# Modulation columns summed on DVE, one product for 32 rows of the special column, one load queue: a spectral block followed by an MLP

## The chip, the cores and the metric

The kernel runs on one core of a Trainium2 chip. The metric is the device time of one execution in microseconds (us). Engines are named as in the profile: PE (TensorE; PEld are its weight loads), DVE (VectorE), ACT (ScalarE), POOL (GpSimd) and SP (SyncE, which here only issues DMAs). SBUF is the core's working memory, PSUM the eight banks into which PE writes; a `bank` in the code is one of them (128 partitions x 512 float32), taken in turn from two of one tag (A, B, C or D).

## The reference

One sequence of 2048 rows by 512 columns, float32. From a condition vector c come six modulation vectors of 512: shift, scale and gate of two blocks.

```python
mod = (silu(c) @ w_mod).reshape(1, 6, 1, 512)
sa, ca, ga, sb, cb, gb = (mod[:, i] for i in range(6))
h = layernorm(x) * (1 + ca) + sa
x = x + ga * irfft2(rfft2(h) * (w_r + 1j * w_i))      # over rows and columns
h = layernorm(x) * (1 + cb) + sb
x = x + gb * (mish(h @ w1 + b1) @ w2)                 # 512 -> 1376 -> 512
```

## The kernel before

The rows are split as 128 x 16 (partition p, tile n), the columns as 128 x 4. The Fourier transforms are products with constant matrices. Where a line has high and low parts ("split"), a float32 is written as a rounded value and its rest, and three products take the place of one. A plain float32 product of 128 x 128 shows as two matmul rows of the profile, one for each pass; transposes show as one.

**Stage 1** (L291-370) goes over the 16 tiles n. `p1_row` (L203) multiplies the transposed tile by the row matrix that `scale_rows` has scaled with 1 + ca (`krs`); `p1_mean` (L213) takes the mean away on DVE, with the row sums `kb` from `row_sums` (L208); `p1_cast` (L218) makes the high part on ACT; the low part comes from POOL for n in `POOL_LOW` (1, 3, ..., 13) and otherwise from DVE in `p1_low` (L231); `p1_col` (L237) is the column product, three sets of three matmuls, of which the third takes the low part; `p1_save` (L247) is ACT's copy into `a_sb`. `norm_sums` (L111) makes a tile's statistics on DVE; `first_guess` (ACT) and `first_scale` (three DVE steps) make its 1/sigma, for two tiles at a time after the first two. `p1_split` (ACT, POOL) splits the column matrices. The order of all engines' work is written out by hand (`manual_schedule`): each engine takes its own instructions in the order of the lines, and so does each DMA queue.

Ahead of tile 0, sigmoid(c) is made with an exp on ACT and three DVE steps (`sc`, 512 values as 128 x 4), eight products of ones by ones run (`warm`, L286), and 16 products of `w_mod`'s scale part by `sc` give 1 + ca's row in four banks (`scale_sums`, L250). c and two of the four pieces of `w_mod` are loaded by ACT's queue, all else by SP's.

The shift sa enters as one more row: `shift_sum` (L261) adds four pieces of `w_mod` (`wms`), each times its column of `sc`, on DVE at tiles 10 to 13; `shift_columns` (L269) turns the 128 partial sums into columns with four products by ones (in `mod_columns`, L105); `shift_rows` (L272) multiplies the row matrix with these columns, picks each partition's own part and adds it up on DVE into `saz`. Both stand ahead of the column products of tiles 14 and 15. `saz` is added by POOL to one column of each group in stage 2 (`p2_shift`, L462).

**Stage 2** (L372-595) goes over 17 groups of frequencies, in the order `seq`; group 0, the fifth, is the special one (frequencies 0 and 256 of the columns, functions `z_*`). For each group: transposes on PE (`p2_in`, L454), a copy on ACT, `saz` on POOL, a product (`p2_mul`, L475), two DVE multiplications with the weights (`p2_prod`, L491), sums on DVE or POOL (L496, L497), transposes back (`p2_back`, L508), a copy on ACT, a product (`p2_out`, L521), and ACT's copies into `d` (`store_d`). Steps are lagged: at step s the loop makes prod(s), mul(s+1), in(s+3), back(s-2), out(s-3). Eight `p2_in` and two `p2_mul` run ahead of the loop. In the special group, `reflected` (L396) makes three matmul pairs per operand: the operand, its first column into one row, and the operand reversed. `z_back` gives two operands, 128 rows (times `kv`) and 32 rows (times `kw`).

The other four modulation vectors are summed in this stage, at most two DVE steps per loop step (`mod_late`, L98 and L100): ga into `modr[:, 0]`, sb into `modr[:, 1]`, cb into `modr[:, 0]`, gb into `modr[:, 2]`. `mod_shift` (L543) turns sb and cb into columns, each with four products by ones, at steps 11 and 18; `mod_gate` (L551) and `apply_gate` (L556) spread ga and gb.

**Stage 3** (L655-675, L898-930) is the inverse transform: `p3_col` and `p3_row` per tile on PE, the addition to x (L674) and the new statistics on DVE, with the splits of w1 and w2 in between (`split_w2`, L715; `split`, L711, is an ACT copy and a DVE subtraction, L713). For w2's tile 3, sums of pieces from POOL (`tsum` = `modr[:, 0:2]`) are split at step 14. **Stage 4** is the MLP, eight pairs of tiles, six steps each: `up` (L748, L750), `front`, `back` (mish), `halves`, `down` (L793, L801).

Of the kernel before, what the change touches and what calls it, by code (L numbers as in the profile page):

```python
# [27 lines left out]
POOL_LOW = range(1, 15, 2)  # L28
# [3 lines left out]
def tile_spectral_block(ctx: ExitStack, tc: tile.TileContext, x_d, w1_d, b1_d, w2_d,  # L32
# [36 lines left out]
    macc = modr[:, 1]  # L69
# [21 lines left out]
    kw = pw.tile([32, 384], F32, name="kw")  # L91
# [10 lines left out]
    def mod_columns():  # L102
        ps = bank("D")
        for j in range(4):
            nc.tensor.matmul(ps[:, j:j + 1], macc[:, j * P:(j + 1) * P], ones[:, 0:1], start=True, stop=True)  # L105
        return ps[:, 0:4]
# [70 lines left out]
    def load_rest():  # L177
        nc.sync.dma_start(ident, kp_d)
# [82 lines left out]
    def shift_sum(k):  # L261
        w, one = wms[:, k, :], sc[:, k:k + 1]
        if k == 0:
            st["sum"] = bank("D")
            nc.vector.tensor_scalar(st["sum"], w, one, 0.0, op0=ALU.mult, op1=ALU.add)
        else:
            nc.vector.scalar_tensor_tensor(macc if k == 3 else st["sum"], w, one, st["sum"], op0=ALU.mult, op1=ALU.add)

    def shift_columns():  # L269
        nc.scalar.mul(cols[:, 0, 0, :], mod_columns(), 128.0)  # L270

    def shift_rows():  # L272
# [5 lines left out]
        pick = modr[:, 1, 0:8]  # L278
# [12 lines left out]
    with tc.manual_schedule():  # L291
        def load_scale(eng, k):
            eng.dma_start(wmc[:, k, :], wm_d[:, 1, k, :])

        nc.scalar.dma_start(sc, c_d.rearrange("b (p k) -> p (b k)", k=4))
        load_scale(nc.scalar, 1)
        load_scale(nc.scalar, 3)
        nc.scalar.preload_act_table_set("natural_log_exp_and_others")
        load_xt(0)
        load_scale(nc.sync, 0)  # L300
        load_scale(nc.sync, 2)
        nc.sync.dma_start(kr, kr_d)
        load_x(0)
        load_m(0)
        for n in range(1, 8):
            load_all(n)
# [8 lines left out]
        warm(8)  # L315
        cps = [bank(t) for t in "CCBB"]
        for k in range(4):
            scale_sums((k,), cps)
        norm_sums(0)
        first_guess(0, 1)  # L320
        scale_rows(cps)
        first_scale(0, 1)
        p1_split(0)
        row_sums()
# [15 lines left out]
        for n in range(N2):  # L340
            if n >= 1:
                p1_save(n - 1)
            if n + 2 < N2:
                p1_row(n + 2)
                if n + 10 < N2:
                    load_all(n + 10)
                if n == 4:
                    nc.sync.dma_start(wms, wm_d[:, 0, :, :])
                if n == 6:
                    load_rest()  # L350
# [17 lines left out]
            if 10 <= n < 14:  # L368
                shift_sum(n - 10)
        p1_save(N2 - 1)  # L370

# [24 lines left out]
    def reflected(out, srcs):  # L396
        for i, (t, w) in enumerate(srcs):
            nc.tensor.matmul(out, t[:, 0:P], w(0), start=(i == 0), stop=False)
            nc.tensor.matmul(out[0:1], t[:, 0:1], w(2), start=False, stop=False)
            nc.tensor.matmul(out, t[:, P:2 * P], w(1), start=False, stop=(i == len(srcs) - 1))  # L400
# [9 lines left out]
    def z_mul():  # L410
        z = st.pop(("z", 0))
        pb = bank("B")
        reflected(pb[:, 0:160], [(z, lambda i: kf[:, 128 + 160 * i:288 + 160 * i])])
        st["pb", 0] = pb

    def z_prod():
# [10 lines left out]
        nc.gpsimd.tensor_tensor(y[:, 80:160], pr[0][:, 80:160], pr[1][:, 0:80], op=ALU.add)  # L427
        st["y", 0] = y

    def z_back():  # L430
# [3 lines left out]
        nc.tensor.transpose(pc[0:32, P:2 * P], y[:, P:P + 32], ident)  # L434
        t1, t2 = buf("t"), buf("t")
        turned(t1, pc[:, 0:P])
        turned(t2[0:32], pc[0:32, P:2 * P])
        st["t", 0] = t1, t2

    def z_out():  # L440
        t1, t2 = st.pop(("t", 0))
        pe = bank("D")
        reflected(pe[:, 0:P], [(t1, lambda i: kv[:, 128 + i * P:256 + i * P]),
                               (t2[0:32], lambda i: kw[:, i * P:(i + 1) * P])])
# [83 lines left out]
    for i, s in enumerate(when):  # L528
        work_mod[s].append((i // 4, (0, 1, 0, 2)[i // 4], nc.vector, i % 4))

    def mod_fetch(s):
        for which, row, eng, k in work_mod.get(s, ()):
            w = late[which, k] = hring.tile([P, 512], F32, name="wm", tag="ht", bufs=4)
            nc.sync.dma_start(w, wm_d[:, 2 + which, k, :])

    def mod_late(s):
        for which, row, eng, k in work_mod[s]:
            mod_step(modr[:, row], late.pop((which, k)), k, eng)

    def mod_shift(i):  # L540
        ps = bank("A")
        for j in range(4):
            nc.tensor.matmul(ps[:, j:j + 1], modr[:, 1 - i, j * P:(j + 1) * P], ones[:, 0:1], start=True, stop=True)  # L543
        if i:
            plus_one(cols[:, 1, i, :], ps[:, 0:4])
        else:
            nc.scalar.copy(cols[:, 1, i, :], ps[:, 0:4])
# [13 lines left out]
    with tc.manual_schedule():  # L561
        for i in range(8):
            nc.sync.dma_start(wqb[:, i], wq_d[8 + i])
        for i in range(LEAD):
# [4 lines left out]
            if i in (3, 5):  # L569
                p2_mul(seq[i // 2 - 1])  # L570
        for s in range(len(seq) + 3):
# [16 lines left out]
            if s == 7:  # L588
                mod_gate()
            if s == 9:  # L590
# [124 lines left out]
    def split_w2(t, sums):  # L715
# [5 lines left out]
        if sums:  # L721
# [208 lines left out]
    front(1)  # L930
    halves(0, back(0))
# [29 lines left out]
def _constants():  # L961
# [80 lines left out]
    kw = np.concatenate([m[128:] for m in zero], 1)  # L1042
# [5 lines left out]
def _layout(x, w_r, w_i, w_mod):  # L1048
# [13 lines left out]
    m = w_mod.reshape(128, 4, 6, 512).transpose(0, 2, 1, 3).copy()  # L1062
    m[:, 0:3] = m[:, 0:3].reshape(128, 3, 4, 128, 4).swapaxes(3, 4).reshape(128, 3, 4, 512)
# [31 lines left out]
```

## Time and profile before

| | us |
|---|---|
| median of 3 runs (lowest to highest) | 396.13 (395.94 to 396.22) |
| the profiled execution | 395.79 |
| its span, first to last instruction | 393.8 |
| busy: PE, DVE, ACT, POOL | 386.4, 297.9, 247.6, 94.2 |
| first matmul of stage 3 (L661) | 102.99 |
| first products of the MLP's second layer (L793) | 154.82 |

An execution takes 2.0 us more than its span. A row of a timeline gives start and duration in us, engine, line, operation, output and inputs by their names in the program, shapes and count; in square brackets stands how long the engine had been idle and what ended it. A row of the waits gives who waited for whom, the sum in us, how often, and the longest. Rows of the windows give the stretch, its length, and the busy time and number of instructions, then the granted clock, the DMA share and GB/s. Rows of the DMA issues give target and source, queue, count, size and the median us from issue to landing. Instructions that follow each other on one engine overlap a little, so the step from start to start (their pitch) is shorter than the duration.

### The profile page before, as it was taken

Reading aid. Unit: us, or ns where it says so; the run is one execution under the profiler, and the core shown is the slowest. Engines: PE = TensorE matmul, PEld = TensorE weight load, DVE = VectorE, ACT = ScalarE, POOL = GpSimd, SP = SyncE. Lnnn points to the kernel's source line nnn. Section 1 sums busy time; section 2 is a strip of 40 time slices with the busy share of each in tenths; the row PEclk is TensorE's granted clock in tenths of the full one; section 3 lists DMA queues with packets and bytes.
Section 4 is the critical chain, followed back from the end, with each engine's and each line's share of the span. In section 5 each row is a group of like instructions: output and inputs, shape, how many; then the busy total and the mean of one; then the engine's idle time right before and its main releaser. Section 6 shows DMA issues by size and latency. Waiting matters only on the chain.

```text
span 393.8 us, 7439 instructions
## 1 busy us (share of the span) xinstructions
PE 386.4 (98%) x2776; PEld 358.5 (91%) x2776; DVE 297.9 (76%) x654; ACT 247.6 (63%) x546; POOL 94.2 (24%) x131
## 2 busy tenths in 40 slices
PE   8999999999999999999999999999999999999996
PEld 8999878899999998998999999999899899899984
DVE  2998858677089998896965965865875974987994
ACT  2788645577657755985674674675674584594751
POOL 0687435566065553120000000000000010017000
PEclk9999999999999999999999999999999999999999
DMA  8999962381214421100100100100100100023011
GB/s 293 377 338 373 318 253 84 87 339 53 83 47 126 137 81 29 54 2 0 55 0 2 54 2 0 56 0 2 53 2 2 49 27 0 25 69 123 1 55 53
DMA packets 20580, 36.45 MB, mean 93 GB/s; under 512 B 3680, under 2 KB 6528, under 8 KB 20160
## 3 DMA queue, kind: packets, MB, share of 16 engines
q1 hardware_dynamic: 20112, 35.45, 26.1%
q8 instruction: 22, 0.36, 0.4%
q10 hardware_dynamic: 432, 0.53, 0.4%
q14 instruction: 14, 0.11, 0.1%
HBM read 31.78 MB, written 4.19 MB: 91 GB/s over the span
## 4 chain that ended last, share of the span: by engine, by line
PE 79%; DVE 11%; DMA 6%; ACT 2%; issue 2%; SPq 0%; POOL 0%
PE bank L801 24%; PE bank L748 20%; PE bank L750 10%; PE bank L521 4%; PE bank L475 3%; DVE st L113 3%; DMA x<-in_A_x_dram 3%; PE bank L793 3%; PE bank L200 2%; PE bank L813 2%; DVE x L674 2%; DMA wms<-in_w_mod_dram 2%; PE bank L508 2%; PE bank L454 2%; PE bank L640 2%
## 5 line engine op out<-in xcount | busy, mean ns | idle before, releaser
L758 ACT ACTIVATE buf<-bank,b1n 128x256 f32<-128x256 f32 (+1 forms) x88 | 40.8, 471 | 67.1 <-PE bank L750 67.0
L759 DVE TENSOR_TENSOR buf<-buf,bank 128x256 f32<-128x256 f32 (+1 forms) x88 | 35.4, 417 | 39.0 <-ACT buf L758 39.0
L713 DVE TENSOR_TENSOR al<-buf,ah 128x512 fp32r<-128x512 f32 (+2 forms) x85 | 53.4, 652 | 1.8 <-ACT ah L712 1.8
L748 PE MATMUL bank<-h2e,w1h 128*128 128x512 f32 (+1 forms) x176 | 48.4, 397 | 0.0
L748 PE MATMUL bank<-h2o,w1h 128*128 128x512 f32 (+1 forms) x176 | 48.3, 396 | 0.0
L730 POOL TENSOR_TENSOR buf<-buf,modr 128x512 f32<-128x512 f32 (+1 forms) x3 | 3.9, 1293 | 183.6 <-DVE buf L759 147.1
L712 ACT CAST ah<-buf 128x512 fp32r<-128x512 f32 (+2 forms) x85 | 43.0, 549 | 0.7 <-DVE buf L775 0.6
L775 DVE TENSOR_TENSOR buf<-buf 128x128 f32<-128x128 f32 x148 | 39.3, 307 | 3.5 <-ACT buf L765 2.2
L765 ACT ACTIVATE buf<-buf 128x512 f32<-128x512 f32 (+1 forms) x48 | 28.6, 596 | 14.8 <-DVE buf L759 14.8
L801 PE MATMUL bank<-w2a,ah 128*128 128x256 f32 x161 | 34.9, 286 | 0.0
L748 PEld LDWEIGHTS bank<-h2o,w1h 128*128 128x128 f32 (+1 forms) x176 | 30.2, 187 | 4.5
L748 PEld LDWEIGHTS bank<-h2e,w1h 128*128 128x128 f32 (+1 forms) x176 | 30.1, 187 | 4.5
L801 PE MATMUL bank<-w2b,ah 128*128 128x256 f32 x147 | 31.8, 283 | 0.0
L750 PEld LDWEIGHTS bank<-h2e,w1l 128*128 128x128 f32 (+1 forms) x176 | 26.7, 185 | 4.2
L750 PEld LDWEIGHTS bank<-h2o,w1l 128*128 128x128 f32 (+1 forms) x176 | 26.7, 185 | 4.2
L750 PE MATMUL bank<-h2e,w1l 128*128 128x256 f32 (+1 forms) x176 | 27.8, 280 | 0.0
L750 PE MATMUL bank<-h2o,w1l 128*128 128x256 f32 (+1 forms) x176 | 27.8, 280 | 0.0
L801 PEld LDWEIGHTS bank<-w2a,ah 128*128 128x128 f32 x161 | 26.7, 191 | 0.0
L113 DVE BATCH_NORM_STATS2 st<-x 128x6 f32<-128x512 f32 x32 | 22.0, 689 | 3.7 <-DMA x<-in_A_x_dram 3.3
L662 PE MATMUL bank<-kc,d 128*128 128x128 f32 x128 | 24.8, 275 | 0.0
L661 PE MATMUL bank<-kc,d 128*128 128x128 f32 x128 | 24.7, 275 | 0.0
L801 PEld LDWEIGHTS bank<-w2b,ah 128*128 128x128 f32 x147 | 24.6, 191 | 0.0
(227 smaller groups left out, 1005.5 us busy)
## 6 DMA issues: line engine op xcount, KB each, us to landing
buf<-in_B_w_dram SPq DMA_DIRECT2D x20, 256.0 KB, 2.7
xring<-in_x_t_dram SPq DMA_DIRECT2D x16, 256.0 KB, 4.4
x<-in_A_x_dram SPq DMA_DIRECT2D x16, 256.0 KB, 4.7
wm<-in_w_mod_dram SPq DMA_DIRECT2D x16, 256.0 KB, 4.4
out_dram<-x SPq DMA_DIRECT2D x7, 512.0 KB, 2.6
mraw<-in_km_dram SPq DMA_DIRECT2D x16, 128.0 KB, 4.5
wqa<-in_w_q_dram SPq DMA_DIRECT2D x8, 256.0 KB, 4.1
wqb<-in_w_q_dram SPq DMA_DIRECT2D x8, 256.0 KB, 5.0
```

The lines of the kernel that those rows point to most:

```text
L113: nc.vector.bn_stats(t, x[:, n, :])
L661: nc.tensor.matmul(o, dj[:, 0:128], kc[0][:, n, :], start=True, stop=False)
L662: nc.tensor.matmul(o, dj[:, 64:192], kc[1][:, n, :], start=False, stop=True)
L712: nc.scalar.copy(h, r)
L713: nc.vector.tensor_tensor(l, r, plain(h), op=ALU.subtract)
L748: nc.tensor.matmul(ps, w1h[:, k, fs], h[:, k], start=(k == 0), stop=False)
L750: nc.tensor.matmul(ps[:, 0:256], w1l[:, k, fs], h[:, k, 0], start=False, stop=(k == 3))
L758: nc.scalar.activation(o, ps[:, 256:], AF.Identity, bias=b1n[:rows, f:f + 1])
L759: nc.vector.tensor_tensor(o, o, ps[:, 0:256], op=ALU.add)
L765: nc.scalar.activation(o, o, AF.Mish)
L775: nc.vector.tensor_tensor(o, p, q, op=op)
L801: nc.tensor.matmul(o, a[p][:, e], w2[t][q][:, r], start=(own and half == 0 and t == 1 and i == 0), stop=(end and i == 2 and (n, half) != ( ...
```

## The change

- **Columns on DVE.** The layout on the host turns `w_mod`'s parts for sa, sb and cb, so that a partition holds an output column and the 512 elements along it are the inputs. `scale_spread` puts `sc` of all 512 inputs on every partition (four products with the identity, then an ACT copy to `scb`), and `mod_column` multiplies and adds up along the row in one DVE instruction with an accumulated output. `shift_sum` does so at tiles 11 to 14, `mod_late` for sb and cb. `mod_columns`, `shift_columns` and `mod_shift` are gone.
- **`shift_rows`** stands behind the last column product and its save.
- **The start.** All loads go by SP's queue in a new order, with `ident` early and each `xt` one tile ahead; six products of warm-up instead of eight; the scale rows and row sums stand ahead of tile 0's statistics; tile 1's low part moves from POOL to DVE.
- **The special column.** The 32 rows are repeated three times (96), turned in one transpose into one operand that holds the straight, reversed and first-column parts, and multiplied in one product with a stacked `kw`.
- **Stage 2's lead-in:** the second `p2_mul` stands behind the fifth `p2_in`, not behind the sixth.
- **w2:** for tile 3's sums, the DVE subtraction of the split moves from step 14 of stage 3 to behind the MLP's first two `front`s.

```diff
-POOL_LOW = range(1, 15, 2)
+POOL_LOW = range(3, 15, 2)
...
-    macc = modr[:, 1]
+    scb = modr[:, 1]
...
-    kw = pw.tile([32, 384], F32, name="kw")
+    kw = pw.tile([96, P], F32, name="kw")
...
-    def mod_columns():
+    def scale_spread():
         ps = bank("D")
-        for j in range(4):
-            nc.tensor.matmul(ps[:, j:j + 1], macc[:, j * P:(j + 1) * P], ones[:, 0:1], start=True, stop=True)
-        return ps[:, 0:4]
+        for k in range(4):
+            nc.tensor.matmul(ps[:, k * P:(k + 1) * P], sc[:, k:k + 1].to_broadcast([P, P]), ident,
+                             start=True, stop=True)
+        st["scb"] = ps
+
+    def mod_column(w, out, by, waste):
+        nc.vector.scalar_tensor_tensor(waste, w, by, scb, op0=ALU.mult, op1=ALU.mult, accum_out=out)
...
     def shift_sum(k):
...
+        mod_column(wms[:, k, :], cols[:, 0, 0, k:k + 1], 128.0, bank("D"))
...
-        nc.scalar.dma_start(sc, c_d.rearrange("b (p k) -> p (b k)", k=4))
-        load_scale(nc.scalar, 1)
-        load_scale(nc.scalar, 3)
+        nc.sync.dma_start(sc, c_d.rearrange("b (p k) -> p (b k)", k=4))
         nc.scalar.preload_act_table_set("natural_log_exp_and_others")
-        load_xt(0)
-        load_scale(nc.sync, 0)
-        load_scale(nc.sync, 2)
+        for k in range(4):
+            nc.sync.dma_start(wmc[:, k, :], wm_d[1, k])
         nc.sync.dma_start(kr, kr_d)
         load_x(0)
+        load_xt(0)
+        nc.sync.dma_start(ident, kp_d)
+        load_xt(1)
         load_m(0)
         for n in range(1, 8):
-            load_all(n)
+            load_x(n)
+            if n < 7:
+                load_xt(n + 1)
+            load_m(n)
...
-        warm(8)
+        warm(6)
         cps = [bank(t) for t in "CCBB"]
         for k in range(4):
             scale_sums((k,), cps)
+        scale_rows(cps)
+        row_sums()
         norm_sums(0)
         first_guess(0, 1)
-        scale_rows(cps)
         first_scale(0, 1)
         p1_split(0)
-        row_sums()
         p1_row(0)
         load_all(8)
         p1_row(1)
         load_all(9)
+        scale_spread()
+        p1_mean(0)
+        p1_cast(0)
         norm_sums(1)
         first_guess(1, 2)
-        p1_mean(0)
-        p1_cast(0)
+        p1_split(1)
+        nc.scalar.copy(scb, st.pop("scb"))
+        p1_low(0)
+        p1_mean(1)
         first_scale(1, 2)
-        p1_split(1)
-        p1_mean(1)
         p1_cast(1)
-        p1_low(0)
         p1_split(2)
         norm_sums(2)
...
-                    nc.sync.dma_start(wms, wm_d[:, 0, :, :])
+                    nc.sync.dma_start(wms, wm_d[0].rearrange("k p e -> p k e"))
...
-            if n == 14:
-                shift_columns()
-            if n == 15:
-                shift_rows()
             p1_col(n)
...
-            if 10 <= n < 14:
-                shift_sum(n - 10)
+            if 11 <= n < 15:
+                shift_sum(n - 11)
         p1_save(N2 - 1)
+        shift_rows()
...
-    def reflected(out, srcs):
...
+    def reflected(out, t, w, more=()):
+        nc.tensor.matmul(out, t[:, 0:P], w(0), start=True, stop=False)
+        nc.tensor.matmul(out[0:1], t[:, 0:1], w(2), start=False, stop=False)
+        for a, b in more:
+            nc.tensor.matmul(out, a, b, start=False, stop=False)
+        nc.tensor.matmul(out, t[:, P:2 * P], w(1), start=False, stop=True)
...
+        nc.gpsimd.tensor_copy(y[:, 160:256].rearrange("p (i k) -> p i k", i=3),
+                              y[:, P:P + 32].unsqueeze(1).to_broadcast([P, 3, 32]))
...
-        nc.tensor.transpose(pc[0:32, P:2 * P], y[:, P:P + 32], ident)
+        nc.tensor.transpose(pc[0:96, P:2 * P], y[:, 160:256], ident)
         t1, t2 = buf("t"), buf("t")
         turned(t1, pc[:, 0:P])
-        turned(t2[0:32], pc[0:32, P:2 * P])
+        nc.gpsimd.memset(t2[0:96, 0:P], 0.0)
+        nc.scalar.copy(t2[0:32, 0:P], pc[0:32, P:2 * P])
+        nc.vector.tensor_copy(t2[32:64, 1:P], pc[32:64, 2 * P - 1:P:-1])
+        nc.scalar.copy(t2[64:96, 0:1], pc[64:96, P:P + 1])
...
+            if which in (1, 2):
+                mod_column(w, cols[:, 1, which - 1, k:k + 1], 1.0, w)
+            else:
+                mod_step(modr[:, 0 if which == 0 else 2], w, k, nc.vector)
...
-            if i in (3, 5):
-                p2_mul(seq[i // 2 - 1])
+            if i in (3, 4):
+                p2_mul(seq[i - 3])
...
-            if s == 11:
-                mod_shift(0)
             mod_late(s)
-            if s == len(seq) + 1:
-                mod_shift(1)
...
+            if s == 14:
+                plus_one(cols[:, 1, 1, :], cols[:, 1, 1, :])
...
-        if sums:
+        if t == 3 and sums:
+            nc.scalar.copy(h[:, 768:], tsum.rearrange("p e d -> p (e d)"))
+        elif sums:
...
     front(1)
+    h, l = (w.rearrange("p e d -> p (e d)")[:, 768:] for w in w2[3])
+    nc.vector.tensor_tensor(l, tsum.rearrange("p e d -> p (e d)"), plain(h), op=ALU.subtract)
     halves(0, back(0))
```

More of the change, by code (lines that the diff above doesn't have):

```diff
@@ L177, in load_rest @@
     def load_rest():
-        nc.sync.dma_start(ident, kp_d)
         nc.sync.dma_start(kf, kf_d)
@@ L261, in shift_sum @@
     def shift_sum(k):
[L262 to L270, printed above, removed]
+        mod_column(wms[:, k, :], cols[:, 0, 0, k:k + 1], 128.0, bank("D"))
     def shift_rows():
@@ L277, in shift_rows @@
                              kr[:, j, :].rearrange("p (c q) -> p c q", c=2), start=True, stop=True)
-        pick = modr[:, 1, 0:8]
+        pick = small.tile([P, 8], F32, name="pick")
         nc.vector.tensor_reduce(pick, ident.rearrange("p (n e) -> p e n", e=8), axis=mybir.AxisListType.X,
@@ L394, in turned @@
         nc.gpsimd.memset(dst[:, P:P + 1], 0.0)
-    def reflected(out, srcs):
[L397 to L400, printed above, removed]
+    def reflected(out, t, w, more=()):
[4 more added lines that the diff above has]
+        nc.tensor.matmul(out, t[:, P:2 * P], w(1), start=False, stop=True)
     def z_in():
@@ L412, in z_mul @@
         pb = bank("B")
-        reflected(pb[:, 0:160], [(z, lambda i: kf[:, 128 + 160 * i:288 + 160 * i])])
+        reflected(pb[:, 0:160], z, lambda i: kf[:, 128 + 160 * i:288 + 160 * i])
         st["pb", 0] = pb
@@ L442, in z_out @@
         pe = bank("D")
-        reflected(pe[:, 0:P], [(t1, lambda i: kv[:, 128 + i * P:256 + i * P]),
-                               (t2[0:32], lambda i: kw[:, i * P:(i + 1) * P])])
+        reflected(pe[:, 0:P], t1, lambda i: kv[:, 128 + i * P:256 + i * P], [(t2[0:96, 0:P], kw)])
         store_d(pe, 0, 1)
@@ L528, in tile_spectral_block @@
     for i, s in enumerate(when):
-        work_mod[s].append((i // 4, (0, 1, 0, 2)[i // 4], nc.vector, i % 4))
+        work_mod[s].append((i // 4, i % 4))
     def mod_fetch(s):
-        for which, row, eng, k in work_mod.get(s, ()):
+        for which, k in work_mod.get(s, ()):
             w = late[which, k] = hring.tile([P, 512], F32, name="wm", tag="ht", bufs=4)
-            nc.sync.dma_start(w, wm_d[:, 2 + which, k, :])
+            nc.sync.dma_start(w, wm_d[2 + which, k])
     def mod_late(s):
[L537 to L547, printed above, removed]
+        for which, k in work_mod[s]:
+            w = late.pop((which, k))
+            if which in (1, 2):
+                mod_column(w, cols[:, 1, which - 1, k:k + 1], 1.0, w)
+            else:
+                mod_step(modr[:, 0 if which == 0 else 2], w, k, nc.vector)
     def mod_gate():
@@ L1041, in _constants @@
     kv = np.concatenate([bwd(4, backward)] + [m[:128] for m in zero], 1)
-    kw = np.concatenate([m[128:] for m in zero], 1)
+    kw = np.concatenate([m[128:] for m in zero], 0)
     out = dict(kr=kr.reshape(128, 4, 128), km=km.reshape(128, 16, 256), kc=kc,
@@ L1061, in _layout @@
     wq = wq.reshape(2, 128, 4, 16, 16, 4).transpose(4, 1, 0, 2, 3, 5).reshape(16, 128, 2, 64, 4)
-    m = w_mod.reshape(128, 4, 6, 512).transpose(0, 2, 1, 3).copy()
-    m[:, 0:3] = m[:, 0:3].reshape(128, 3, 4, 128, 4).swapaxes(3, 4).reshape(128, 3, 4, 512)
+    m = w_mod.reshape(128, 4, 6, 512).transpose(2, 1, 0, 3).copy()
+    m[1:3] = m[1:3].reshape(2, 4, 128, 128, 4).swapaxes(3, 4).reshape(2, 4, 128, 512)
+    t = w_mod.reshape(128, 4, 6, 512).transpose(2, 3, 1, 0).reshape(6, 512, 512)
+    m[0] = t[0].reshape(128, 4, 512).swapaxes(0, 1)
+    m[3:5] = t[3:5].reshape(2, 4, 128, 512)
     xt = x.reshape(128, 16, 128, 4).transpose(1, 2, 3, 0)
```

2 lines of the change are left out of this document (removed).

## The prediction

> **What bounds the kernel now.** I read the page first, then the waits of TensorE (PE) from 8 to 160 us.
>
> ```profile
> PE 386.4 (98%) x2776; PEld 358.5 (91%) x2776; DVE 297.9 (76%) x654; ACT 247.6 (63%) x546; POOL 94.2 (24%) x131
> PE 79%; DVE 11%; DMA 6%; ACT 2%; issue 2%; SPq 0%; POOL 0%
> ```
>
> ```profile
> PE bank L398 <- DVE buf L491: 0.8, 1, 0.8
> PE bank L454 <- ACT a_sb L248: 0.7, 1, 0.7
> PE bank L793 <- ACT ah L712: 0.4, 1, 0.4
> PE bank L242 <- DVE buf L235: 0.3, 1, 0.3
> PE bank L105 <- DVE modr L267: 0.2, 1, 0.2
> ```
>
> PE is busy 98% of the span, and from 8 to 160 us it waits only five times, 2.4 us in all. The chain of waits names DVE and DMA for 17%, but what they delay is never PE by more than these rows. So the time is PE's list of products plus these waits: a product removed counts in full, unless PE then catches up with another engine. Everything below is counted on PE's queue.
>
> **1. The start.** The timelines of PE, DVE and ACT, two rows of the DMA issues, L253's part of the window from 5.8 to 9.2 us, and a row of the chain:
>
> ```profile
> 1.05 3.78 PE L289 MATMUL bank<-ones 128*128 128x128 f32 x16 [1.05 <-DVE b1n L309]
> 4.90 4.23 PE L253 MATMUL bank<-sc,wmc 128*128 128x128 f32 x32
> 9.23 1.29 PE L200 MATMUL bank<-modr,ones 128*128 128x128 f32 x8
> 13.06 0.50 PE L242 MATMUL bank<-buf,mring 128*128 128x512 f32 x1
> ...
> 8.83 1.15 DVE L258 SCALAR_TENSOR_TENSOR modr<-kr,bank 128x128 f32<-128x128 f32 x4
> 13.30 0.74 DVE L235 SCALAR_TENSOR_TENSOR buf<-bank,rstd,buf 128x512 fp32r<-128x512 f32 x1
> 13.96 0.68 DVE L113 BATCH_NORM_STATS2 st<-x 128x6 f32<-128x512 f32 x1
> ...
> 15.57 0.72 DVE L215 SCALAR_TENSOR_TENSOR bank<-modr,mv,bank 128x512 f32<-128x512 f32 x1
> 16.20 0.15 DVE L126 SCALAR_TENSOR_TENSOR ve<-mv,bank 128x2 f32<-128x2 f32 x1
> 16.66 0.69 DVE L113 BATCH_NORM_STATS2 st<-x 128x6 f32<-128x512 f32 x1
> ...
> 10.55 0.59 ACT L211 COPY modr<-bank 128x512 f32<-128x512 f32 x1 [0.85 <-PE bank L200]
> ...
> sc<-in_c_dram ACTq DMA_DIRECT2D x1, 2.0 KB, 3.1
> out_dram<-x SPq DMA_DIRECT2D x2, 256.0 KB, 2.0
> 5.80:9.20 3.40, 3.33 (x30) 3.14 (x28) 1.00 1.03 373
> 19.65 0.89 PE bank L200 x8
> ```
>
> A pass costs 0.21 us before 5.8 us (L289) and 0.112 after. The 2 KB of sc, now alone at the head of one queue, can land up to 1.1 us sooner (3.1 against 2.0 us); I take 0.7. The scale products then start near 4.1 instead of 4.9, run eight passes slow and 24 fast, and end near 8.5 instead of 9.0. The four scale rows (L258) no longer wait for tile 0's statistics, so the row sums end near 9.5 instead of 10.3: -0.8. The six warm-up products end just before. On SP's queue kr and tile 0 now stand behind two more scale loads, and ident (64 KB, 0.17 us at the window's 373 GB/s) ahead of xt1; xt0, no longer first, pays for both, and all of it is wanted only after 8.5. ACT's copy of scb lies under row products. The spread adds eight passes, +0.9. So column product 0 still starts near 13.0.
>
> DVE now decides. Pitches from the rows: low part (L235) 0.66, statistics 0.80 (two between 13.96 and 15.57), mean (L215) 0.63, three scale steps 0.46. ACT copies the row sums (L211) before it makes tile 0's guess, so the first scale steps start near 10.6. Up to the low part of tile 1, taken from POOL, DVE has three scale steps, three means, three statistics and two low parts: 1.4 + 1.9 + 2.4 + 1.3 = 7.0, hence 17.6. PE wants it at 13.0 + 1.4 + 0.9 + 0.9 = 16.2: column product 1 loses 1.4 us, and the next row product waits behind it. Part of that (0.4) replaces small waits up to 19.65. Net **+0.75**. Bounds: -0.4 if DVE starts earlier, +1.5 if sc is no sooner.
>
> **2. The end of stage 1.** PE and DVE again:
>
> ```profile
> 37.85 1.05 PE L200 MATMUL bank<-modr,xring 128*128 128x128 f32 x8
> 45.62 1.05 PE L105 MATMUL bank<-ones,modr 128*128 128x1 f32 x8 [0.18 <-DVE modr L267]
> 48.04 1.05 PE L276 MATMUL bank<-kr,cols 128*128 128x128 f32 x8
> 50.22 0.28 PE L244 MATMUL bank<-buf,mring 128*128 128x256 f32 x1
> 51.17 2.31 PE L454 MATMUL bank<-ident,a_sb 128*128 128x128 f32 x15 [0.68 <-ACT a_sb L248]
> ...
> 37.73 0.75 DVE L265 TENSOR_SCALAR bank<-wms,sc 128x512 f32<-128x512 f32 x1 [0.29 <-DMA wms<-in_w_mod_dram]
> 49.85 1.04 DVE L284 TENSOR_REDUCE saz<-modr 128x64 f32<-128x512 f32 x1
> ...
> L100 DVE SCALAR_TENSOR_TENSOR modr<-wm,sc,modr x12: 728/792/1225, 62.1 to 95.8; 128x512 f32<-128x512 f32 x12
> ```
>
> From row product 13 (37.85) to the last column product (50.50) pass 12.65 us. Gone are L105 (1.05), L276 (0.89, moved behind), and waits of 0.45. Four sums stay on DVE, but one tile later, with an accumulated output that no row shows. The same operation on two SBUF tensors takes 0.73 (L100), a reduction of 512 elements 1.04 (L284). I take the row with the same operands and a small readout, a pitch of 0.80; bounds 0.65 and 1.04. In the clock of the kernel before, DVE is free at 37.44 and has, up to the last low part, four means, two scale steps, two statistics, three low parts, four sums and 0.2 of waiting: 2.5 + 0.9 + 1.6 + 2.0 + 3.2 + 0.2 = 10.4 us, to 47.9. PE, with 2.3 us per tile from 37.85 on and nothing between, would start column product 14 at 44.7; its high part comes at 44.95, its low part at 46.4 instead of 45.9, so it ends at 46.9, the low part of 15 comes just as it is wanted, and column product 15 ends at 48.3: **-2.2** (-2.65 and -1.2 at the bounds). The same walk with 0.65 or 1.04 per sum gives the bounds. wms as four 2 KB pieces per partition is covered: its first use moves behind 39.5.
>
> **3. Into stage 2.** The shift rows' four products now fill the 0.68 that PE waited for ACT, 0.2 past it. Behind them come two DVE operations (0.7 and 1.04), then POOL's shifts, which wait for saz: 0.9 + 0.1 + 0.7 + 1.05 + 0.3 = 3.05 us behind the last column product, and only then the first L475, which now starts after 2.8 (its fifteen transposes begin at 51.17): +0.2. The second L475 group moves ahead of the sixth transposes, which no longer give ACT's copies time, +0.25. The chain of the first wait row follows:
>
> ```profile
> 57.48 1.52 POOL L497 TENSOR_TENSOR buf<-buf 128x192 f32<-128x192 f32 x2
> 58.35 1.29 DVE L491 TENSOR_TENSOR buf<-bank,wqa 128x512 f32<-128x512 f32 x2 [0.48 <-POOL buf L497]
> ```
>
> POOL's first L497 sits behind the last early shift, so L491 and the special column's L398 slip alike: **+0.45** (0 to +0.8).
>
> **4. Stage 2.** PE, DVE and POOL:
>
> ```profile
> 72.39 0.48 PE L398 MATMUL bank<-kw,buf 32*128 32x128 f32 x2
> 73.52 1.12 PE L551 MATMUL bank<-modr,ones 128*128 128x512 f32 x2
> 98.88 0.95 PE L543 MATMUL bank<-ones,modr 128*128 128x1 f32 x8
> 99.69 0.71 PE L508 MATMUL bank<-ident,buf 128*128 128x128 f32 x4
> ...
> 95.78 1.23 DVE L100 SCALAR_TENSOR_TENSOR modr<-wm,sc,modr 128x512 f32<-128x512 f32 x1
> 98.37 0.94 POOL L497 TENSOR_TENSOR buf<-buf 128x256 f32<-128x256 f32 x1 [1.92 <-DVE buf L491]
> ```
>
> The kw products go from 1.13 (72.39 to 73.52) to two passes, 0.22 to 0.35: **-0.85**. The added POOL copy and memset, one ACT copy and DVE's copy lie a step ahead of it; uncovered they cost about 0.5. Each group of column products (L543) is 0.81. The first goes in full: **-0.81**. The second doesn't: the last transposes (L508, 99.69) need POOL's result, ready at 99.31, so pulling them to 98.88 buys about **-0.34**; DVE's order ahead of POOL (L100, L491) hangs on an earlier transpose and moves with PE. Eight column sums replace scaling steps on DVE; its idle time there hides them.
>
> **5. The w2 split.**
>
> ```profile
> 146.70 1.19 DVE L713 TENSOR_TENSOR w2a<-modr,w2hi 128x1024 fp32r<-128x1024 f32 x1
> 154.80 0.56 DVE L713 TENSOR_TENSOR al<-buf,ah 96x256 fp32r<-96x256 f32 x1 [1.51 <-ACT ah L712]
> ```
>
> PE's only wait near it is 0.4 (L793). The subtraction leaves the DVE chain to it and moves past three tiles' additions and statistics into DVE's 1.51 of idling. POOL's next w2 differences wait for it until about 154; their reader comes 9 us later. **-0.4** (0 to -0.45).
>
> **The sum:** 0.75 - 2.2 + 0.45 - 0.85 - 0.81 - 0.34 - 0.4 = -3.4. Stages 3 and 4 shift as a whole: PE runs there without other waits. The profiled execution took 395.79 (span 393.8 and 2.0 around it), which gives 392.4; the median of the runs, 396.13, is 0.34 above it, which gives 392.7.
>
> **Rivals.**
>
> [...]
>
> [...]
>
> *Stage 2 gives nothing.* PE would wait for POOL or DVE where it now multiplies, as at the last transposes; -2.0 is lost, 394.7. Against it: PE waits for neither between 61 and 103 us, and for the first two savings the results lie over 2 us ahead.
>
> *Slower than before: one queue carries too little.* Place: every tile of stage 1. A tile loads 640 KB in PE's 2.3 us, 285 GB/s; below that PE waits for xt or x. At 240 GB/s a tile takes 2.73, and 16 tiles lose 6.9 us: 399.6. Slower than before from about 263 GB/s on. Against it: 373 GB/s moved from 5.8 to 9.2 us, with all but 0.53 MB of the kernel's loads on SP's queue already.
>
> **How the numbers follow.** The forecast (392.7, its own range 391.8 to 393.6) has 0.57; half rate 0.15; the late clock 0.07; stage 2 without gain 0.10; the slow queue 0.03; 0.08 is left for several of my unknowns falling badly together, among them the start. A measurement of this kernel tells about 0.2% (0.8 us) from no change. Faster by that means under 395.3: the forecast, half rate, and most of the late clock and of stage 2, 0.85. Same takes the rest of those two and half of what is left, 0.09; slower 0.06. The range: the low end adds the sums' low bound (-0.45), no wait at the last transposes (-0.45) and an earlier DVE (-0.4) to the forecast, 391.4; the high end takes in half rate and most of the two rivals at 394.7, so 394.8.
>
> **What would show it.** Start: L253 begins near 4.1 and row product 5 (19.65 before) 0.75 later, with PE waiting about 1.4 for DVE's low part of tile 1. Stage 1: the last column product ends near 49.1, the sums' pitch near 0.8. The special column's first product (59.79) near 58.8. The first stage 3 product (102.99) near 100. L793 without a wait. Wrong it is if the sums take over 1.2, if PE still runs at 0.21 per pass after 6 us, or if new waits of PE over 1 us stand between 60 and 100 us.

## The result, and the profile after

The changed kernel takes 393.0 us (median of 6 runs, 392.45 to 393.36) against 396.23 (6 runs, 395.94 to 398.77) of the kernel before: a ratio of 0.990, 95% interval 0.9875 to 0.993. The forecast was 392.7. The profiled execution took 392.9 with a span of 391.0, where the sum had given 392.4. The total is right; several of its terms are not.

The page of the changed kernel, engines and chain of waits:

```profile
PE 382.9 (98%) x2752; PEld 355.5 (91%) x2752; DVE 299.5 (77%) x667; ACT 247.7 (63%) x545; POOL 94.8 (24%) x131
PE 89%; DVE 5%; ACT 2%; DMA 1%; issue 1%; POOL 1%; SPq 0%; POOLq 0%; ACTq 0%
```

PE has 3.5 us less to do, and the span is 2.8 shorter. The chain now names DVE and DMA for 6% where it named them for 17%. The waits of PE from 8 to 160 us (who waits for whom: total, times, longest) are these:

```profile
PE bank L245 <- DVE buf L238: 1.5, 1, 1.5
PE bank L391 <- DVE buf L490: 0.8, 1, 0.8
PE bank L507 <- POOL buf L496: 0.3, 1, 0.3
PE bank L453 <- ACT early L456: 0.2, 1, 0.2
```

Of the five waits of before only the special column's 0.8 (now L391) is left. The other three are new; the 1.5 and the 0.3 had been forecast. The timeline of the changed kernel at the start, PE first, then ACT and DVE:

```profile
1.05 2.93 PE L284 MATMUL bank<-ones 128*128 128x128 f32 x12 [1.05 <-DVE b1n L304]
3.93 4.75 PE L256 MATMUL bank<-sc,wmc 128*128 128x128 f32 x32
8.52 1.23 PE L203 MATMUL bank<-modr,ones 128*128 128x128 f32 x8
...
13.08 0.48 PE L245 MATMUL bank<-buf,mring 128*128 128x512 f32 x1
18.03 0.50 PE L245 MATMUL bank<-buf,mring 128*128 128x512 f32 x1 [1.45 <-DVE buf L238]
20.89 0.83 PE L203 MATMUL bank<-modr,xring 128*128 128x128 f32 x6
...
2.40 0.20 ACT L306 ACTIVATE sg<-sc 128x4 f32<-128x4 f32 x1 [0.38 <-DMA sc<-in_c_dram]
10.76 0.16 DVE L130 SCALAR_TENSOR_TENSOR ve<-mv,bank 128x1 f32<-128x1 f32 x1 [0.73 <-ACT bank L123]
16.10 0.72 DVE L218 SCALAR_TENSOR_TENSOR bank<-modr,mv,bank 128x512 f32<-128x512 f32 x1
17.22 0.75 DVE L238 SCALAR_TENSOR_TENSOR buf<-bank,rstd,buf 128x512 fp32r<-128x512 f32 x1
```

The scale products (L256) start at 3.93, right behind the warm-up; column product 0 at 13.08; the last part of column product 1 stands 1.45 for the low part that DVE makes from 17.22 on; row product 5 comes at 20.89. The end of stage 1 and the lead-in of stage 2, same view:

```profile
39.32 1.05 PE L203 MATMUL bank<-modr,xring 128*128 128x128 f32 x8
41.06 0.67 DVE L110 SCALAR_TENSOR_TENSOR bank<-wms,modr 128x512 f32<-128x512 f32 x1
41.66 0.14 DVE L110 DVE_READ_ACCUMULATOR bank<-wms,modr 128x1 f32 x1
41.66 0.75 DVE L218 SCALAR_TENSOR_TENSOR bank<-modr,mv,bank 128x512 f32<-128x512 f32 x1
49.44 0.28 PE L247 MATMUL bank<-buf,mring 128*128 128x256 f32 x1
...
57.49 1.27 POOL L496 TENSOR_TENSOR buf<-buf 128x192 f32<-128x192 f32 x2
58.11 1.29 DVE L490 TENSOR_TENSOR buf<-bank,wqa 128x512 f32<-128x512 f32 x2 [0.63 <-POOL buf L496]
59.55 0.51 PE L391 MATMUL bank<-kf,early 128*128 128x160 f32 x2 [0.80 <-DVE buf L490]
```

A sum with an accumulated output (L110) is followed 0.60 later by the next DVE operation; its readout (0.14) costs DVE nothing there. Last, the special column's products, the last transposes of stage 2, and products of the MLP's second layer (L787, the first and the third):

```profile
71.70 0.49 PE L394 MATMUL bank<-kw,buf 96*128 96x128 f32 x2
72.03 0.39 PE L395 MATMUL bank<-kv,buf 128*128 128x128 f32 x2
72.25 1.02 PE L545 MATMUL bank<-modr,ones 128*128 128x512 f32 x2
...
97.08 0.75 PE L507 MATMUL bank<-ident,buf 128*128 128x128 f32 x4 [0.33 <-POOL buf L496]
...
151.68 0.50 PE L787 MATMUL bank<-w2b,ah 96*128 96x512 f32 x1
152.48 0.50 PE L787 MATMUL bank<-w2b,al 96*128 96x512 f32 x1
```

The same marks in both timelines, with the shift that the prediction's running sum gives:

| PE's mark | before | after | shift | predicted |
|---|---|---|---|---|
| row sums | 9.23 | 8.52 | -0.71 | -0.8 |
| column product 0 | 13.06 | 13.08 | +0.02 | 0 |
| row product 5 | 19.49 | 20.89 | +1.40 | +0.75 |
| row product 13 | 37.85 | 39.32 | +1.47 | +0.75 |
| special column's first product | 59.79 | 59.55 | -0.24 | -1.0 |
| gate product (L551, now L545) | 73.52 | 72.25 | -1.27 | -1.85 |
| last transposes of stage 2 | 99.69 | 97.08 | -2.61 | |
| first product of stage 3 | 102.99 | 100.42 | -2.57 | -3.0 |
| M: the product behind the MLP's first products of its second layer (L793, now L787) | 156.45 | 153.51 | -2.94 | -3.4 |
| span | 393.8 | 391.0 | -2.8 | -3.4 |

### The profile page after: what moved, and what is told of

Same layout as the page of the kernel before. It is cut to its first block, busy times and chain, and to the rows that moved or that the text cites. A ratio compares the mean times of both kernels' runs of the same rounds, so it can differ in the third digit from the quotient of the medians.

```text
span 391.0 us, 7384 instructions
## 1 busy us (share of the span) xinstructions
PE 382.9 (98%) x2752; PEld 355.5 (91%) x2752; DVE 299.5 (77%) x667; ACT 247.7 (63%) x545; POOL 94.8 (24%) x131
## 4 chain that ended last, share of the span: by engine, by line
PE 89%; DVE 5%; ACT 2%; DMA 1%; issue 1%; POOL 1%; SPq 0%; POOLq 0%; ACTq 0%
PE bank L795 24%; PE bank L742 20%; PE bank L744 10%; PE bank L203 4%; PE bank L474 3%; PE bank L520 3%; PE bank L663 3%; PE bank L245 3%; PE bank L654 3%; PE bank L653 3%; PE bank L787 2%; PE bank L807 2%; PE bank L632 2%; PE bank L507 2%; PE bank L246 1%; PE bank L453 1%
```

## The experiments

The start differs between executions of one program by more than most terms (row sums between 7.97 and 9.20, below), and the medians here don't tell 0.3 us apart. So a time is given with each kernel, but tenths are read as distances between two marks of one trace, both behind the start.

**One operation back on POOL.**

```diff
-POOL_LOW = range(3, 15, 2)
+POOL_LOW = range(1, 15, 2)
```

> The changed kernel with tile 1's low part back on POOL. Theory (column product 1 waits because the low part of tile 1 is the last of a full DVE queue, 17.22 to 17.97): ACT now writes a plain copy of tile 1 first (0.69) and the high part 0.62 later, so column product 1 begins near 15.9 instead of 15.37; POOL, busy with tile parts to 16.4, then needs 1.3 to 1.7 and has the low part at 17.4 to 17.9. The wait of 1.45 shrinks to 0.5 to 1.0, and row product 5 comes at 20.3 to 20.8 instead of 20.89; the end moves by -0.1 to -0.6. Rival (it is DVE's whole backlog and not this one operation): tile 2's low part or its mean is late instead, and row product 7 (25.50) does not move.

392.9 us (ratio to the kernel before 0.992, 0.990 to 0.994). This execution began late: column product 0 at 13.77, 0.69 behind the changed kernel's. Row product 5 is nevertheless only 0.02 behind (20.91), and row product 7 (25.77) 0.27. PE's timeline:

```profile
16.69 0.50 PE L245 MATMUL bank<-buf,mring 128*128 128x512 f32 x1 [0.36 <-ACT buf L228]
18.05 0.50 PE L245 MATMUL bank<-buf,mring 128*128 128x512 f32 x1 [0.16 <-POOL buf L229]
```

Counted from column product 0 the edit gives 0.67 up to row product 5 and, after 0.25 lost again at the next tile, 0.43 from row product 7 on. So undoing this one move recovers less than half of what PE loses there; the high part from ACT (0.36) and the low part from POOL (0.16) are now waited for instead.

**The scale pieces on two queues.**

```diff
-        for k in range(4):
-            nc.sync.dma_start(wmc[:, k, :], wm_d[1, k])
+        nc.scalar.dma_start(wmc[:, 1, :], wm_d[1, 1])
+        nc.scalar.dma_start(wmc[:, 3, :], wm_d[1, 3])
+        nc.sync.dma_start(wmc[:, 0, :], wm_d[1, 0])
+        nc.sync.dma_start(wmc[:, 2, :], wm_d[1, 2])
```

> The changed kernel with the second and fourth piece of the scale weights on ACT's queue, behind its table load. Theory (one queue issues each piece 0.47 later than the last, so the scale products stop for the third piece at 6.28 until 6.63): the pieces land closer together, sc 0.5 later without effect since the warm-up passes run to 3.77 anyway; row sums start at 8.2 to 8.4 instead of 8.52 and everything behind moves by as much, -0.1 to -0.3. Rival (the memory, not the queue, is slow there: between 4.0 and 5.0 us the window moves far less than the 390 GB/s around it): no change at the row sums, within 0.1.

393.07 us (0.994, 0.991 to 0.997), and neither theory: the row sums came at 10.72, 2.2 later. The vector c landed 2.4 us after its issue instead of 1.6, so the exp came at 3.18 instead of 2.40; the first piece landed later, too, and PE stood idle from 3.77 to 4.96. Its passes then stayed slow. Windows of this kernel (duration, then busy time and count of instructions for PE, PEld, DVE, ACT, POOL):

```profile
4.00:5.00 1.00, 0.04 (x1) 0.07 (x1) 0.00 (x0) 0.00 (x0) 0.00 (x0) 1.00 1.08 412
8.00:9.00 1.00, 1.00 (x7) 1.00 (x6) 0.00 (x0) 0.00 (x0) 0.00 (x0) 1.00 1.06 389
10.00:11.00 1.00, 1.00 (x11) 1.00 (x10) 0.75 (x3) 0.00 (x0) 0.00 (x0) 1.00 1.07 372
```

Between 8 and 9 us seven passes of PE are counted, between 10 and 11 eleven; single passes are 0.21 apart up to 9.36 and 0.11 behind it. That is the late pace that the prediction's chances call the late clock, and an idle PE (1.2 us) goes ahead of it here. (The granted clock reads 1.00 in all these windows: what the trace shows is the pace of the passes.) Of the five runs three took 392.9 to 393.1 and may have escaped it; the trace is of one of the other two (395.2).

**Fewer warm-up products**, to test that by itself: `warm(6)` becomes `warm(3)`.

> The changed kernel with three warm-up products instead of six, so that PE stands idle from 2.5 to 3.9 us. [...] Rival (the pace depends on the time since the first pass, 4.2 us after it in the changed kernel): fast passes near 5.3 and no change, within 0.3.

394.76 us (0.996, 0.993 to 0.998). PE idles from 2.5 to 4.14, where it waits for the first piece of `w_mod`; the windows of this kernel:

```profile
3.00:4.00 1.00, 0.00 (x0) 0.00 (x0) 0.34 (x2) 0.00 (x0) 0.00 (x0) 1.00 1.01 373
7.00:8.00 1.00, 1.00 (x7) 1.00 (x6) 0.00 (x0) 0.00 (x0) 0.00 (x0) 1.00 0.98 350
8.00:9.00 1.00, 1.00 (x11) 1.00 (x11) 0.00 (x0) 0.00 (x0) 0.00 (x0) 1.00 1.01 365
```

The fast pace comes near 8.0, 3.8 us after PE began again, the row sums at 9.65, and +1.1 stays to the end. By the rival, 4.2 us after the first pass, it would have been 5.3; that is out.

**POOL's early shifts later.**

```diff
-        if seq.index(g) >= 2:
+        if 2 <= seq.index(g) and seq.index(g) not in (5, 6, 7):
             p2_shift(g)
...
                 p2_prod(seq[s])
+            if s == 0:
+                for g in seq[5:8]:
+                    p2_shift(g)
```

> The changed kernel with POOL's shifts of the last three early groups moved behind POOL's half of the first group's product. Theory (what sets the special column's first product, 59.55, is POOL's first L496 behind the last early shift, as step 3 of the prediction says): POOL's L496 starts near 55.5 instead of 57.49, DVE's third pair of L490 near 57.5 instead of 58.11, and the special column's first product near 58.9; the end moves by -0.4 to -0.6. Rival (ACT's copies or DVE's own list set it): the first product stays within 0.15 of 59.55.

393.56 us (0.993, 0.991 to 0.996). Its start is 0.20 behind the changed kernel's; the special column's first product is 0.38 ahead, and so is everything to the end. The edit gives 0.58. POOL, DVE and PE of this kernel:

```profile
55.72 0.77 POOL L496 TENSOR_TENSOR buf<-buf 128x192 f32<-128x192 f32 x1 [1.06 <-DVE buf L490]
57.74 1.29 DVE L490 TENSOR_TENSOR buf<-bank,wqa 128x512 f32<-128x512 f32 x2
59.17 0.51 PE L391 MATMUL bank<-kf,early 128*128 128x160 f32 x2 [0.29 <-DVE buf L490]
```

POOL's first half product starts at 55.72 instead of 57.49, DVE's third pair follows without a wait, and PE's falls from 0.80 to 0.29: the chain that step 3 named is the one.

**The second early product as before.**

```diff
-            if i in (3, 4):
-                p2_mul(seq[i - 3])
+            if i in (3, 5):
+                p2_mul(seq[i // 2 - 1])
```

> The changed kernel with the second early product behind the sixth transposes again, as before the change. Theory (step 3: the earlier product takes time away from ACT's copies, 0.25): the special column's first product comes 0.1 to 0.4 sooner, 59.15 to 59.45, and the end moves by as much. Rival (the wait for saz alone sets the lead-in): first product within 0.1 of 59.55.

393.38 us (0.993, 0.991 to 0.995). The start is 0.18 ahead of the changed kernel's, the special column's first product 0.56 (58.99): 0.38 from the edit, at the upper end of what the theory allowed. ACT's last early copy starts 0.41 sooner against the last column product, and POOL's L496 behind it 0.52, as the theory has it. At mark M, 0.31 is left.

**Three `kw` products again.**

```diff
-        reflected(pe[:, 0:P], t1, lambda i: kv[:, 128 + i * P:256 + i * P], [(t2[0:96, 0:P], kw)])
+        reflected(pe[:, 0:P], t1, lambda i: kv[:, 128 + i * P:256 + i * P], [
+            (t2[0:32, 0:P], kw[:, 0:P]), (t2[0:32, P:2 * P], kw[:, P:2 * P])], (t2[0:32, 0:1], kw[:, 2 * P:3 * P]))
...
```

The one-row product stands behind that of `kv`, and the copies that stack the rows are gone.

> The changed kernel with the special column's 32 rows as three products again (two passes each, one of them for one row), and without the copies that stack them. Theory (step 4: kw's two further products are on PE's path and count in full): from the special column's first product to the gate product 13.5 to 13.7 us as before the change, instead of 12.70; the first stage 3 product comes 0.8 to 1.0 later against the special column's first product, 41.7 to 41.9 instead of 40.87, and the end as much. Rival (the end of stage 2 waits for POOL anyway, 0.33): only 0.5 to 0.7 arrives there.

393.63 us (0.994, 0.992 to 0.995). From the special column's first product to the gate product it takes 13.42, to the first stage 3 product 41.59 instead of 40.87: +0.72, all of it on the path, none taken up by POOL's wait. The mechanism is the theory's; the size falls between its 0.8 to 1.0 and the rival's 0.5 to 0.7. PE's timeline:

```profile
70.83 0.38 PE L392 MATMUL bank<-kv,buf 128*1 128x128 f32 x2
71.14 0.38 PE L394 MATMUL bank<-kw,buf 32*1 32x128 f32 x2
71.44 0.71 PE L396 MATMUL bank<-kw,buf 32*128 32x128 f32 x4
72.08 0.49 PE L397 MATMUL bank<-kv,buf 128*128 128x128 f32 x2
```

It is 0.31 less than in the kernel before (13.73), with as many products. There the order was three of `kv`, then three of `kw`; here those of one row stand together and those of 32 rows together. In these two lists a pair of passes takes 0.22 behind one of its own form, and 0.30 to 0.42 where the form changes. Up to these products the two PE lists run with the same steps, so the order is all that differs.

**Column products that nobody reads**, at the two old places (after step 11's fetches and ahead of the last transposes):

```diff
+            if s in (11, len(seq) + 1):
+                spare = bank("A")
+                for j in range(4):
+                    nc.tensor.matmul(spare[:, j:j + 1], gbr[:, j * P:(j + 1) * P], ones[:, 0:1], start=True, stop=True)
             mod_late(s)
```

> The changed kernel with two groups of four one-column products whose result nobody reads, at the two places where the kernel before had its column sums in stage 2. Theory (step 4: the first counts in full, the second only for what the last transposes don't wait for POOL anyway): the first delays everything behind it by 0.8, the second the last transposes by 0.35 to 0.5; from the special column's first product to the first stage 3 product 42.0 to 42.2 instead of 40.87, end +1.15 to +1.3. Rival A (both on the path): 42.5, +1.6. Rival B (what stage 2 saves on PE is taken back by DVE or POOL): under +0.5.

394.5 us (0.997, 0.996 to 0.998). PE's timeline:

```profile
82.63 0.95 PE L576 MATMUL bank<-ones,modr 128*128 128x1 f32 x8
97.55 0.95 PE L576 MATMUL bank<-ones,modr 128*128 128x1 f32 x8
98.36 0.70 PE L507 MATMUL bank<-ident,buf 128*128 128x128 f32 x4
```

The first group shifts all that follows by 0.88. Behind the second the last transposes have lost POOL's wait and are 0.32 later, the first stage 3 product 0.27. In all 1.15, at the low end of the theory, and neither rival.

**Each shift sum twice.**

```diff
-        mod_column(wms[:, k, :], cols[:, 0, 0, k:k + 1], 128.0, bank("D"))
+        for _ in range(2):
+            mod_column(wms[:, k, :], cols[:, 0, 0, k:k + 1], 128.0, bank("D"))
```

> The changed kernel with each of the four shift sums made twice, the second over the first. The trace of the changed kernel gives a pitch of 0.60 to 0.61 per sum on DVE. Theory (step 2: DVE's list, not PE, sets the end of stage 1, with the low parts of tiles 14 and 15 used within 0.1 of their end): four more sums bring the last column product 1.8 to 2.4 later against row product 13, 12.2 to 12.8 instead of 10.4, and the end as much. Rival (PE has the longer list there and the sums lie in its cover): under +0.8.

397.91 us (1.006, 1.003 to 1.009). The first product behind the last column product comes 14.17 after row product 13 instead of 10.24: +3.93, twice what the theory gave. DVE does set the end of stage 1, but four more sums cost it 4.06. DVE and POOL of this kernel:

```profile
41.00 0.67 DVE L110 SCALAR_TENSOR_TENSOR bank<-wms,modr 128x512 f32<-128x512 f32 x1
41.77 0.70 DVE L110 SCALAR_TENSOR_TENSOR bank<-wms,modr 128x512 f32<-128x512 f32 x1
...
44.65 1.68 POOL L229 TENSOR_TENSOR buf<-buf 128x512 fp32r<-128x512 f32 x1 [1.09 <-DMA kiv<-in_ki_dram]
45.29 1.59 DVE L110 SCALAR_TENSOR_TENSOR bank<-wms,modr 128x512 f32<-128x512 f32 x1
```

A second sum into the same output starts 0.77 behind the first, not 0.60: here the readout isn't hidden. And the one at 45.29 runs until 46.88, 0.55 after POOL's L229 has ended at 46.33, as if it had stood still beside it. (The four pairs cost 0.79, 1.69, 0.79 and 0.79 more than single sums.)

**The w2 subtraction back in its split.**

```diff
-        if t == 3 and sums:
-            nc.scalar.copy(h[:, 768:], tsum.rearrange("p e d -> p (e d)"))
-        elif sums:
+        if sums:
             split(h[:, 768:], l[:, 768:], tsum.rearrange("p e d -> p (e d)"))
...
-    h, l = (w.rearrange("p e d -> p (e d)")[:, 768:] for w in w2[3])
-    nc.vector.tensor_tensor(l, tsum.rearrange("p e d -> p (e d)"), plain(h), op=ALU.subtract)
```

> The changed kernel with the w2 subtraction back inside the split ahead of the last three column products of stage 3. Theory (step 5: that split delays the high part which the first stage 4 product L787 reads): L787's products start with a wait of 0.3 to 0.4 and the first product behind them comes 0.25 to 0.4 later against the first stage 3 product (53.09 in the changed kernel). Rival (the gain there is only passed on to the later wait for the low part, as PE's third pass, 152.48, already shows): under 0.1.

393.28 us (0.994, 0.992 to 0.996). L787's first product (here L785) comes only 0.10 later, and the product behind them 0.20 *sooner*: 52.90 from the first stage 3 product, where the changed kernel takes 53.09 and the kernel before 53.46. In the changed kernel the moved subtraction makes the low part late (PE's third pass at 152.48) and saves almost no wait: without it L787's counterpart waits 0.06, not the 0.3 to 0.4 of the theory. It is the rival's mechanism, with the opposite sign.

**That move alone, in the kernel before** (the same two hunks, the other way round).

> The kernel before with one part of the change alone: the w2 subtraction moved behind the first two fronts. Theory A (step 5 as predicted): the wait of 0.40 of the first stage 4 product goes and nothing else happens: from the first stage 3 product to the first product behind those of L793, 53.46 in the kernel before, it takes 53.05 to 53.15, and the end -0.4. [...]

395.98 us (0.999, 0.996 to 1.001). The same distance is 53.12, -0.34: the size of theory A. A small DVE step is held here as in the kernel before, 1.23 where such a step takes 0.16 (DVE of this kernel):

```profile
133.09 1.23 DVE L126 SCALAR_TENSOR_TENSOR ve<-ve,rstd 128x4 f32<-128x4 f32 x1
```

So there were two ways to end the same wait. In the kernel before, DVE's second scale step fell beside POOL's split of w1:

```profile
132.36 1.27 POOL L620 TENSOR_TENSOR w1l<-buf,w1h 128x512 fp32r<-128x512 f32 x1 [2.16 <-ACT w1h L619]
132.39 1.26 DVE L126 SCALAR_TENSOR_TENSOR ve<-ve,rstd 128x4 f32<-128x4 f32 x1
134.78 1.41 DVE L713 TENSOR_TENSOR w2a<-modr,w2a 128x1024 fp32r<-128x1024 f32 x1
```

With the subtraction put back into the changed kernel, POOL's split starts 0.49 sooner against PE, the first step is held (0.95) instead of the second (0.16), and L713's counterpart takes 1.19 instead of 1.41. DVE is then 0.49 less behind PE than in the kernel before, and most of the wait is gone without the move. The 0.49 goes back to a load. Some steps ahead of POOL's split, ACT casts another piece of w1 and waits for its load (first row: the kernel before; second: the subtraction put back):

```profile
127.84 0.62 ACT L619 CAST w1h<-buf 128x512 fp32r<-128x512 f32 x1 [0.91 <-DMA buf<-in_B_w_dram]
125.00 0.62 ACT L611 CAST w1h<-buf 128x512 fp32r<-128x512 f32 x1 [0.40 <-DMA buf<-in_B_w_dram]
```

In both kernels this piece is issued 21.8 behind the first stage 3 product (at 124.78 and 122.45); ACT has it 3.06 and 2.55 later, and ACT's work from there up to POOL's split is shifted by that difference. The kernel before with the move alone takes 3.04, the changed kernel 2.73. The other kernels with the change lie between 2.55 and 2.76, but the one with the unread products takes 3.04, so whether the change brings the sooner landing or the execution does is open.

**Four edits together:** tile 1's low part on POOL, the late shifts, the old order of the early products, the w2 subtraction in its split.

> The changed kernel with four edits together: tile 1's low part on POOL, the last three early shifts behind POOL's first half product, the second early product behind the sixth transposes, the w2 subtraction back in its split. Theory (each takes off what it took off alone, measured from the start of column product 0: 0.43, 0.58, 0.30 to 0.38 and 0.20): 1.0 to 1.6 less than the changed kernel behind the start, 391.4 to 392.0. The second and third edit shorten the same wait of 0.8, so together they can give at most about 0.9. Rival (DVE is the bound in the lead-in and the two overlap fully): 1.2 in all at most, and a wait of the special column's product stays.

392.73 us (391.75 to 394.11; ratio 0.990, 0.987 to 0.994): by the times not to be told from the changed kernel. This execution started late (row sums at 8.93). From column product 0 to mark M it takes 139.20, the changed kernel 140.44: -1.24, within the theory's range. The rival's 1.2 with a wait that stays nearly fits that sum as well (0.2 of the wait is left); against it, the second and third edit give 0.76 together, less than 0.58 + 0.38 but more than either alone. The w2 subtraction's return gives 0.04 instead of 0.20, and a wait for the high part (0.3) is back. PE's waits in this kernel:

```profile
PE bank L788 <- ACT ah L707: 0.3, 1, 0.3
...
PE bank L391 <- DVE buf L490: 0.2, 1, 0.2
```

## Why the prediction was right, and where it was wrong

The total owes something to luck. At mark M the sum is off by +0.46, from +0.72 at the start, -0.05, +0.09, -0.33 and +0.03 in the four terms behind it, so its largest error was in part made up by another one. And the medians lie 3.23 apart, the two profiled executions that the marks come from only 2.89.

**The start: wrong in size, +1.40 for +0.75.** The steps were right one by one: scale products at 3.93 (4.1 predicted), row sums -0.71 (-0.8), column product 0 unmoved, then a wait for DVE's low part of tile 1. What was mis-sized is DVE's list and what PE loses by it, and the step's own terms, 1.4 less 0.4, make 1.0 and not the 0.75 it states. The low part ended at 17.97, not 17.6: the list began at 10.76 instead of 10.6 and took 7.2 instead of 7.0. PE wanted it at 16.41 and lost 1.62 and 0.1 more to start again, where 1.4 was counted. Another 0.16 is a reading error of mine: 19.65 for row product 5 was its place in the chain of waits, while the timeline of before has it at 19.49. Putting that low part on POOL recovers 0.43. The rest was there before it: DVE comes to tile 2's mean at 16.10 where it came at 15.57, since its list begins behind the scale rows and ACT's copy of the row sums (10.76 for 9.89). No run undoes that order. That sc is ready earlier than any bound I gave (exp at 2.40, before 3.87) bought no more, since PE was in its warm-up until 3.77 and, with a shorter one, waits until 4.14 for the first piece of `w_mod`.

**The end of stage 1: -2.25 for -2.2, by two errors.** A sum costs 0.60, under my low bound of 0.65, at which the walk gave -2.65. On PE's side the walk was 0.4 short: column product 14 starts 0.13 late for its high part and goes on 0.17 late for its low part, with a slower pass behind each, too short for the list of waits; and I let the last column product take 1.4, where the end of its last pass (49.72) lies 1.58 behind its start. Doubling the sums confirms that DVE has no slack there: 4.06 more on DVE came through as 3.93. The half rate that the chances and the high end of the range count with no run shows: the trace has a pitch of 0.60 with accumulation and two float32 inputs in SBUF, against 0.66 for the low parts, which have one input in PSUM and no accumulation.

**The lead-in: +0.54 for +0.45** (59.55 against 59.79, with the last column product's end moved from 50.50 to 49.72). Both mechanisms held: POOL's L496 behind the last shift (0.58 when taken away) and the early product that takes time from ACT's copies (0.38 for my 0.25). They share one wait. The 0.58 is what taking three shifts out of the chain gives, not what the later saz had cost; that part of the +0.54 wasn't measured alone.

**Stage 2: -2.33 for -2.0.** The `kw` term was too small, -1.03 for -0.85: from the special column's first product to the gate product 12.70 instead of 13.73. Two products are worth 0.72; the other 0.31 is that PE's passes change form less often, which I had not counted. The first column group gave 0.88 (-0.81 predicted, and as much when put back), the second 0.32 (-0.34), with the 0.33 wait for POOL that the step named; the last 0.10 is the gate product itself (1.02 for 1.12). The rival in which stage 2 gives nothing is out.

**The w2 split: -0.37 for -0.4, and the reason fails.** The step said that the subtraction's leaving the DVE chain ends PE's 0.4. Alone in the kernel before it gives 0.34. But in the changed kernel the wait would have gone without it, and the move there costs 0.2. The effects aren't additive: with the other three edits the same undoing gave 0.04. In these traces it matters how DVE's steps fall beside POOL's, and that follows the landing of one load; no run moves that load alone. So part of this term may be chance of the execution.

Beside the DVE step held until 133.65, POOL's operation ends at 133.63; in the doubled sums POOL's ends at 46.33 and the sum has 0.55 left. By what a DVE operation is held there no run shows.

**The other rivals.** The late clock didn't come in the profiled execution, but the late pace is real: an idle PE of 1.2 and of 1.6 us ahead of the scale products brought it, at +2.2 (about half of that the idling itself) and +1.1. The pace came 4.4 and 3.8 us after the restart. No run of the changed kernel shows the 394.7 that the high end of the range has for a late clock; these two losses, each brought by an edit, stand in its place. One queue was enough: PE waits for no load between 8 and 160 us. (By the rival's own terms, 640 KB per tile, the break-even is about 261 GB/s and not 263.)

## What to carry to other kernels

Count what an edit puts on an engine that is already behind, to the end of its list: the row sums came 0.71 sooner, but with DVE's list begun later and one 0.66 us operation longer, PE stood 1.45 and ended the start 1.4 later. Before crediting an edit with a wait that is gone, undo it in the changed kernel and also make it alone in the old one; here the move gained 0.34 in the old one and cost 0.20 in the new one. Where a start varies between executions, measure tenths between marks behind it.

## What was not expected of the hardware

- **The start varies.** Nine kernels with the same program up to the row sums had them between 7.97 and 9.20 us (8.52 in the changed kernel's profile). In part the fast pace came at other times behind the same warm-up: at 0.21 and 0.112 a pass, the first 16 scale passes put it by my estimate near 4.5 us on the clock of the span with the four edits (2.02 us from 4.36 on), 5.0 with the low part on POOL (2.41 from 3.99 on) and 5.1 with the subtraction put back (2.53 from 3.91 on); in part a scale piece landed late (PE waited 0.91 for one in the kernel with the low part on POOL). A late start stayed: with the scale pieces on two queues the row sums came 2.20 later and the span was 2.1 longer, with three warm-up products 1.13 and 1.0.
- **A DVE operation of 0.16 us took 1.26** beside one of POOL (1.27) in the kernel before, with two operands in SBUF; the statistics, which read one, took their usual 0.69 beside POOL's next one. Which of the small steps was held went with the start of POOL's operation: at 132.36 in the kernel before, as the first step ends, it was the second; 0.3 to 0.5 sooner against PE it was the first (1.11 in the changed kernel, 0.95 with the subtraction put back).
- **A sum's readout** (0.14) was free before an unrelated operation (pitch 0.60) and not before a sum into the same output (0.77). Two sums into different outputs, in stage 2 of the changed kernel (76.92 and 77.56), followed each other after 0.64.
- **A change of form between products cost 0.1 to 0.2 per pair of passes** in the kernel before and with three `kw` products (0.30 to 0.42 against 0.22, one row, 32 rows and 128). Between 96 rows and 128 none shows in the changed kernel: 0.11 from the last `kw` pass (71.92) to the next one of `kv` (72.03).
